# Loading w1 in two parts instead of four runs, with a new instruction order, in a fused S5 scan and gated MLP kernel

## The chip, the cores and the metric

The kernel runs on one core of one Trainium2 chip. The metric is the time of one execution on the device, in microseconds (us); the median of the runs counts. One execution is also recorded by the hardware profiler; its span, from the first to the last instruction, is shorter than the time of the whole execution, which has some start and end around it.

The engines have their own instruction streams and run in order: PE (TensorE, matrix products; PEld is its weight load), DVE (VectorE), ACT (ScalarE), POOL (GpSimd) and SP (SyncE, which here only issues DMAs). An instruction that waits for a semaphore holds back everything behind it on its own engine.

## What is computed

The reference, cut to its core (L = 2048 rows, D = 448, F = 1792, all inputs bf16):

```python
xn = layernorm(x)
# part A: a diagonal complex state of size 448, scanned over the rows
Lam_bar = exp(exp(log_dt) * (Lambda_re + 1j * Lambda_im))
Bu = xn @ (((Lam_bar - 1) / Lam)[:, None] * (B_re + 1j * B_im)).T
h[t] = Lam_bar * h[t - 1] + Bu[t]
s = 2 * (h @ (C_re + 1j * C_im).T).real + xn * Dskip
# part B: an MLP on a second layernorm
g = silu(gelu(layernorm(xn) @ w1 + b1) @ w2 + b2)
out = x + s * g
```

## The kernel before, in words

The rows go through in 4 groups of 512, each group in 2 blocks of 256 rows; a block holds 128 pairs of an even and an odd row. A group passes through these stages, named here as in the rest of the text, with their lines:

- **Layernorm.** DVE takes statistics (L395, L401; for group 0 L425, L426), then scales: for group 0 ACT makes the first ones (L428 and L429), for the others POOL or DVE makes a power or a Newton step (L472 to L482, the last of them L482). DVE or ACT normalizes into `xn_sb` for part A and `xn2_sb` for part B (L447 for group 0; L493 on DVE, L494 on ACT). Both are transposed to `xnT` and `xn2T`, by transposing DMAs on SP (L83), except that group 0's part B is transposed on TensorE (L454) and copied from PSUM by DVE or ACT (L413).
- **mm1** (L803). xn2T times w1, 14 column tiles of 128 ("tiles of F") taken in pairs, each pair in two phases of 6 and 8 matmuls. K is 448, so the last 64 rows of K are handled by a second copy: `w1_sb` has in its fourth plane the rows 384 to 447 in partitions 64 to 127, and in partitions 0 to 63 a copy of rows 320 to 383 that DVE makes (L350). A phase needs its PSUM banks free: ACT drains each pair with gelu into `gT` (L807), and those drains come in TensorE's order. Group 0 goes through five pairs for block 0 first, then the pairs 5 and 6 for both blocks, then five pairs for block 1.
- **mm2** (L828). gT times w2, 14 matmuls for each of four quarters of a group, in PSUM banks 5 and 6. DVE adds b2 (L831), ACT applies silu (L833), or tanh (L835) with a DVE step (L836) for the groups in the middle. ACT loads a table when it changes between gelu (L620), silu and sine (L616).
- **The state.** TensorE makes Bu (L731) from xnT and BT, four steps of two products each per group, in bank 4; ACT or DVE copies it to `u_sb` (L413). DVE rotates it (L746 to L750), scans it (L755, twice, and L757), ACT or DVE copies the scan to bf16 (L413, `vs`), DVE rotates back (L773 to L777) into `h_sb`; L777 is the last step, of the half pair of states.
- **y** (L871, L874, L877). h times CZ (even rows, with xn times M0 added) or CQ (odd rows), in bank 7. DVE adds the skip term (L883) and multiplies by g (L885, L888), DVE or POOL adds x (L891), SP stores.

Once, at the start, parameters are prepared: the rotation tables (DVE L626 to L633, then five sines on ACT, L642), the products LB of B (L660, L661, L663 into `Bn`), their transposes BT (DMA), the products CQ and CZ of C (L660, L661, L663), and M0 (L714, L699), which needs all seven CQ, with `De`, the identity times Dskip (L612), added. De lies in the scan's work space and so waits for the last of the sines. The b2 and Dskip rows are loaded by POOL's queue and wait for the last 64-row load of w1.

**The order is written out.** Every step is a task that says which names it reads and writes; `emit` derives the waits from them. `ORDER` lists all tasks in the order in which they are put on their engines' streams, so it alone sets what comes behind what on an engine and on SP's and POOL's queues. `SECOND` lists the tasks that take their second engine (of DVE, ACT and POOL). DMAs have a semaphore each; a reader waits until the whole transfer has landed. SP's queue is in order: a transpose that waits for its source holds back the loads behind it.

**The loads of w1.** `CH` cuts the 14 tiles into runs of 2, 4, 4 and 4. `ldw1(c, ...)` loads run c: one transfer for the rows 0 to 383 (384 row pieces, name `w1_c`), one for the rows 384 to 447 (`w1r_c`), and the copy of 64 rows (`w1c_c`). A phase of mm1 reads the names of its run. SP issues, in this order: x of block 0 (odd half, even half), x of block 1, the 64 rows of run 1, run 1, run 0, its 64 rows, the 64 rows of run 2, run 2, run 3, its 64 rows, x of blocks 2 and 3, the four pieces of w2, and then B and C in turn.

Of the kernel before, what the change touches and what calls it, by code (L numbers as in the profile page):

```python
# [7 lines left out]
ACT = mybir.ActivationFunctionType  # L8
# [145 lines left out]
def dram_ap(t, offset, ap):  # L154
    return bass.AP(tensor=t.tensor, offset=offset, ap=ap)
# [2 lines left out]


ORDER = [int(k) for k in """  # L160
# [17 lines left out]
""".split()]  # L178
SECOND = [int(k) for k in """
46 54 55 62 64 67 70 75 77 84 108 113 131 134 159 161 163 164 166 178 185 186 188 190 191 221 223 225 227 229 231 239 249 250 259 267 269 330 361 363  # L180
364 383 399 400 435 446 467 479 481 486 490 498 500 501 503 509 527 528 608 611
""".split()]


# [14 lines left out]
def bass_recurrent_scan__ssm_conv_s5__mixer_channel_mlp__prompt_kernel(  # L199
# [18 lines left out]
    with ExitStack() as es:  # L218
# [85 lines left out]
        with nc.Block():  # L304
# [26 lines left out]
            def ld(eng, o, i, writes, nbytes, prio, reads=(), dur=0.45):  # L331
                kb.dma(eng, o, i, reads=reads, writes=writes, prio=prio, nbytes=nbytes, dur=dur)
# [9 lines left out]
            CH = ((0, 2), (2, 4), (6, 4), (10, 4))  # L342
            chunk = [c for c, (_, n) in enumerate(CH) for _ in range(n)]

            def ldw1(c, prio):
                a, w = CH[c][0] * 128, CH[c][1] * 128
                ld("sp", w1_sb[:, 0:3, a:a + w], dram_ap(B_w1, a, [[F, 128], [128 * F, 3], [1, w]]), [f"w1_{c}"], 384 * w * 2, prio, dur=0.55)
                ld("sp", w1_sb[64:128, 3, a:a + w], dram_ap(B_w1, 384 * F + a, [[F, 64], [1, w]]), [f"w1r_{c}"], 64 * w * 2, prio)
                low, high = w1_sb[0:64, 3, a:a + w], w1_sb[64:128, 2, a:a + w]
                kb.either(("dve", lambda e: e.tensor_copy(low, high)), ("act", lambda e: e.activation(low, high, ACT.Copy)), [f"w1_{c}"], [f"w1c_{c}"])  # L350

            S1 = 10 * PINNED
            for par in range(0 if 0 else 2):
                ld("sp" if par or not 0 else "act", x_all[:, 0, par, :], dram_ap(A_x, par * D, [[2 * D, 128], [1, D]]), [f"x0p{par}"], 114688, S1)
            ldx(1, 1, S1 + 2)
            ldw1(0, S1 + 1)
            ld("pool", brows[0:3, :], dram_ap(B_b1, 256, [[512, 3], [1, 512]]), ["br0"], 3072, 0, reads=["br"])
            ld("pool", brows[3:4, 0:256], dram_ap(B_b1, 0, [[256, 1], [1, 256]]), ["br1"], 512, 0, reads=["br"])
            for c in (1, 2, 3):
                ldw1(c, S1 + 3)  # L360
            for ri, bm in enumerate((A_B_re, A_B_im)):
                ld("sp", Bn[:, ri * 3:ri * 3 + 3, D:896], dram_ap(bm, 0, [[D, 128], [128 * D, 3], [1, D]]),
                   [f"Bn{ri}"], 344000, S1 + 5, dur=0.9)
# [494 lines left out]
            def ym(g, b, par, prio):  # L858
# [9 lines left out]
                def part(c0, c1):  # L868
                    bk = 7 if g < NG - 1 else (7, 4, 0)[(2 * b + par + (c0 > 0)) % 3]
                    w = c1 - c0  # L870
                    fns = [lambda e, k=k: e.matmul(psum[:, bk, c0:c1], h_sb[:, hb, k, k0:k0 + 128], cm[:, k, c0:c1], start=(k == 0), stop=False)  # L871
                           for k in range(7)]
                    if par == 0:
                        fns += [lambda e, d=d: e.matmul(psum[:, bk, c0:c1], xnT[:, gx, d, xs], M0[:, d, c0:c1], start=False, stop=(d == 3)) for d in range(4)]  # L874
                        du, rk = 2.1, [f"M0{d}" for d in range(4)] + [f"M0{d}d" for d in range(3)] * 1 + [f"CZ{k}" for k in range(7)]
                    else:
                        fns[-1] = lambda e: e.matmul(psum[:, bk, c0:c1], h_sb[:, hb, 6, k0:k0 + 128], cm[:, 6, c0:c1], start=False, stop=True)  # L877
                        du, rk = 1.36 * w / D + (0.05 if w < D else 0), [f"CQ{k}" for k in range(7)]
                    pe(fns, [f"h{hb}", f"hh{hb}", f"hp{hb}"] + ([f"xnT{gx}_{b}"] if par == 0 else []) + rk, [f"ps{bk}"], du, prio + c0 / 1e4)
                    y, ky = psum[:, bk, c0:c1], f"ps{bk}"  # L880
                    if par and not late(n):
                        y, ky = xr[:, b, c0:c1], f"xr{b}"
                        dve(lambda e: e.tensor_tensor(xr[:, b, c0:c1], psum[:, bk, c0:c1], xd[:, g % 2 * 2 + b, c0:c1], ALU.add), [f"ps{bk}", f"xd{g % 2 * 2 + b}"] + ([f"CZ{k}" for k in range(7)] if g == 0 else []), [ky])  # L883
                    if silu_now(g):
                        dve(lambda e: e.scalar_tensor_tensor(out=t3[:, fb, c0:c1], in0=y, scalar=2.0, in1=g_sb[:, gs, c0:c1],  # L885
                                                             op0=ALU.mult, op1=ALU.mult), [ky, f"g{gs}"], [f"t3{fb}_{c0}"])
                    else:
                        dve(lambda e: e.tensor_tensor(t3[:, fb, c0:c1], y, g_sb[:, gs, c0:c1], ALU.mult), [ky, f"g{gs}"], [f"t3{fb}_{c0}"])  # L888
                    far = par and late(n)
                    res = xr[:, b, c0:c1] if far else x_all[:, 2 * g + b, par, c0:c1]  # L890
                    add = lambda e: e.tensor_tensor(o_sb[:, ob, par * D + c0:par * D + c1], t3[:, fb, c0:c1], res, ALU.add)  # L891
                    rd = [f"t3{fb}_{c0}", f"t3{fb}_256"] if c0 == 0 and not (last and par) else [f"t3{fb}_{c0}"]
                    rd += [f"xr{b}"] if far else xk(2 * g + b)
                    on = [("dve", add, 0.1 + (0.28, 0.47)[par] * w / D, 0.12), ("pool", add, 0.2 + 1.1 * w / D, 0.15)]
                    if last and par or 1:
                        kb.either(*on, rd, [f"o{ob}_{par}_{c0}"], prio)
                    else:
                        dve(add, rd, [f"o{ob}_{par}_{c0}"], on[0][2], prio)
                    if last:
                        kb.dma("act" if c0 else "sp", dram_ap(out, off + par * D + c0, [[2 * D, 128], [1, w]]), o_sb[:, ob, par * D + c0:par * D + c1], reads=[f"o{ob}_{par}_{c0}"],  # L900
                               writes=[f"out{g}{b}{par}{c0}"], prio=prio, nbytes=256 * w)
# [119 lines left out]
```

## Time and profile before

| | us |
|---|---|
| median of 3 runs | 153.87 (153.40 to 154.16) |
| the profiled execution, whole | 154.72 |
| its span, first to last instruction | 153.0 |
| PE busy | 147.5 |
| DVE busy | 128.3 |
| ACT busy | 98.4 |
| POOL busy | 40.5 |

Of the span, mm1 (L803) has TensorE busy for 44.7 us, mm2 (L828) for 44.4, Bu (L731) for 24.0. The granted TensorE clock is 1.0 throughout.

How to read the lines in this text. A line of the timeline gives start, length, engine, line, operation, output from inputs, shape, and in brackets the idle time before it with what ended it. A line of the chain of waits gives start, length and what the end of the program was waiting for in that stretch. A group's line gives the count, busy time, mean duration in ns, and the idle time before. A line of the DMA view gives the size of a transfer and the time from its issue to its landing. Instructions of one engine overlap a little, so ends are later than the next start by up to 0.1 us on DVE and ACT.

### The profile page before, as it was taken

The page shows a single profiled execution, that of the slowest core. Times are in us where ns is not written, and L with a number is a line of the kernel's source. Part 1 is how long each engine was busy: PE and PEld are TensorE (multiplying, and loading weights), DVE is VectorE, ACT ScalarE, POOL GpSimd, SP SyncE. Part 2 cuts the span into 40 slices and gives each one's busy share as a digit, 9 for nine tenths or more (in the row PEclk, how much of TensorE's full clock was granted, in tenths as well). Part 3 has the DMA queues.
Part 4 walks back from the last instruction along what each step waited for, and adds up shares of the span by engine and source line. Part 5 has one row for each costly group of instructions (what it writes and reads, how often), then busy time and mean ns, then how long its engine had stood idle before and what let it go on. Part 6 is the DMA issues. An engine that isn't in the chain of part 4 may idle for free.

```text
span 153.0 us, 2990 instructions
## 1 busy us (share of the span) xinstructions
PE 147.5 (96%) x1136; PEld 87.4 (57%) x1136; DVE 128.3 (84%) x270; ACT 98.4 (64%) x182; POOL 40.5 (26%) x100
## 2 busy tenths in 40 slices
PE   7979999999999999999999999999999999999992
PEld 7767755544566567545544556764454666555551
DVE  2839988999998969999999996469968726999984
ACT  3785998968889739997898620453479834067400
POOL 5267843135020920000447006200072031000200
DMA  4899999979996300600003031710331001100022
GB/s 119 239 276 398 282 216 185 182 152 144 170 237 170 58 4 0 132 5 4 0 0 62 4 60 30 167 48 16 60 93 29 4 0 57 63 0 0 4 99 81
DMA packets 31236, 14.73 MB, mean 96 GB/s; under 512 B 24752, under 2 KB 30774, under 8 KB 31222
## 3 DMA queue, kind: packets, MB, share of 16 engines
q1 hardware_dynamic: 30912, 14.26, 40.8%
q0 software_dynamic: 160, 0.23, 0.7%
q8 instruction: 9, 0.15, 0.4%
q10 hardware_dynamic: 150, 0.05, 0.1%
q14 instruction: 5, 0.04, 0.1%
HBM read 6.89 MB, written 1.84 MB: 57 GB/s over the span
## 4 chain that ended last, share of the span: by engine, by line
PE 92%; DMA 3%; DVE 1%; SPq 1%; issue 1%; DVEq 0%
PE psum L803 29%; PE psum L828 28%; PE psum L731 14%; PE psum L871 12%; PE psum L874 4%; DMA w_sb<-in_B_w_dram 3%; PE psum L714 3%; SPq L84 1%; PE psum L877 1%; DVE t L885 1%; DVE tmp L891 1%; PE psum L699 1%; PE psum L454 0%; DVEq L136 0%
## 5 line engine op out<-in xcount | busy, mean ns | idle before, releaser
L803 PE MATMUL psum<-xn2T,w_sb 64*128 64x512 bf16 (+1 forms) x462 | 44.7, 345 | 1.3 <-issue 0.9
L828 PE MATMUL psum<-w_sb,gT 128*128 128x448 bf16 x224 | 44.4, 353 | 0.0
L807 ACT ACTIVATE gT<-psum,b1f 128x512 bf16<-128x512 f32 (+1 forms) x66 | 36.0, 624 | 11.7 <-PE psum L803 11.5
L803 PEld LDWEIGHTS psum<-xn2T,w_sb 64*128 64x128 bf16 x462 | 24.3, 109 | 20.8 <-issue 3.1
L828 PEld LDWEIGHTS psum<-w_sb,gT 128*128 128x128 bf16 x224 | 21.6, 98 | 20.3 <-issue 0.6
L413 ACT ACTIVATE u_sb<-psum 128x512 bf16<-128x512 f32 (+2 forms) x22 | 10.5, 477 | 23.0 <-PE psum L731 22.7
L731 PE MATMUL psum<-xnT,BT 128*128 128x256 bf16 x196 | 24.0, 273 | 0.0
L731 PEld LDWEIGHTS psum<-xnT,BT 128*128 128x128 bf16 x196 | 19.0, 98 | 5.4 <-issue 1.1
L755 DVE TENSOR_TENSOR_SCAN s_w<-dk,vs 128x774 f32<-128x774 f32 x8 | 14.0, 1760 | 0.1
L891 POOL TENSOR_TENSOR tmp<-t,x_all 128x448 bf16<-128x448 bf16 x5 | 5.2, 1032 | 33.1 <-DVE t L888 30.7
L494 ACT ACTIVATE xn_sb<-x_all,lnw 128x448 bf16<-128x448 bf16 (+2 forms) x21 | 13.0, 661 | 1.2 <-DVE xn_sb L493 1.1
L413 ACT ACTIVATE vs<-s_w 64x256 bf16<-64x256 f32 (+2 forms) x16 | 10.9, 682 | 2.6 <-DVE s_w L755 1.5
L871 PE MATMUL psum<-CZ,h_sb 128*128 128x448 bf16 x56 | 11.9, 352 | 0.0
L831 DVE TENSOR_TENSOR o<-psum,b2bc 128x448 f32<-128x448 f32 x16 | 9.8, 615 | 1.2 <-PE psum L828 1.0
L871 PE MATMUL psum<-CQ,h_sb 128*128 128x448 bf16 (+2 forms) x54 | 10.5, 332 | 0.0
L871 PEld LDWEIGHTS psum<-CZ,h_sb 128*128 128x128 bf16 x56 | 5.4, 98 | 4.7 <-DVE lnmv L401 0.4
L871 PEld LDWEIGHTS psum<-CQ,h_sb 128*128 128x128 bf16 x54 | 5.1, 98 | 4.0 <-DVE t L885 0.4
L874 PE MATMUL psum<-M,xnT 128*128 128x448 bf16 x32 | 7.4, 352 | 0.0
L883 DVE TENSOR_TENSOR Cr<-psum,xd 128x448 f32<-128x448 f32 x7 | 4.3, 620 | 3.5 <-PE psum L877 3.4
L395 DVE BATCH_NORM_STATS2 lnst<-x_all 128x6 f32<-128x448 bf16 x12 | 7.0, 615 | 0.2 <-DMA x_all<-in_A_x_dram 0.2
L474 POOL TENSOR_TENSOR lnw<-lnw,mhalf 128x8 f32<-128x8 f32 x3 | 7.0, 2335 | 0.2
L493 DVE TENSOR_SCALAR xn_sb<-x_all,lnw 128x448 bf16<-128x448 bf16 (+2 forms) x19 | 6.9, 396 | 0.0
(160 smaller groups left out, 188.7 us busy)
## 6 DMA issues: line engine op xcount, KB each, us to landing
out_dram<-tmp SPq DMA_DIRECT2D x7, 224.0 KB, 2.0
x_all<-in_A_x_dram SPq DMA_DIRECT2D x3, 448.0 KB, 4.1
w_sb<-in_B_w_dram SPq DMA_DIRECT2D x3, 448.0 KB, 8.6
w_sb<-in_B_w_dram SPq DMA_DIRECT2D x3, 384.0 KB, 6.1
vs<-in_A_C_re_dram SPq DMA_DIRECT2D x1, 392.0 KB, 11.2
Bn<-in_A_B_im_dram SPq DMA_DIRECT2D x1, 336.0 KB, 10.0
Bn<-in_A_B_re_dram SPq DMA_DIRECT2D x1, 336.0 KB, 10.2
vs<-in_A_C_im_dram SPq DMA_DIRECT2D x1, 336.0 KB, 10.2
```

The costliest lines, as they stand in the source:

```text
L395: dve([lambda e, b=b, par=par, q=q: e.bn_stats(lnst[:, q, :], x_all[:, 2 * g + b, par, :])], [f"x{2 * g + b}"] , [f"st{q}"], 0.62, prio)
L413: kb.either(("act", [lambda e, o=o, i=i: e.activation(o, i, ACT.Copy) for o, i in pairs]), ("dve", [lambda e, o=o, i=i: e.tensor_copy(o, i ...
L474: power = fns + [lambda e: e.tensor_tensor(w(2), w(0), mhalf[:].to_broadcast([128, 2, nq]), ALU.pow), lambda e: e.tensor_tensor(w(3), mean ...
L494: ("act", [lambda e, o=o, i=i: e.activation(o, i, ACT.Identity, bias=nb, scale=rs) for o, i in parts], 0.75, 0.2)]
L731: fns = [lambda e, r=r, m=m, d=d: e.matmul(psum[:, 4, r * NK:(r + 1) * NK], BT[:, m, d, :], xnT[:, gx, d, :], start=(d == 0), stop=(d == 6 ...
L755: dve(lambda e, so=so, vi=vi: e.tensor_tensor_scan(so, dk[:].rearrange("p i c -> p (i c)"), vi, 0.0, ALU.mult, ALU.add), ["v", "vl", "dk", ...
L803: return lambda e: e.matmul(view(bk[k]), w1_sb[rows, d, fcol(2 * j + k)], rhs[rows, d, :, :], start=not second and n == 0, stop=second and ...
L807: act([lambda e, k=k: e.activation(gT[:, gb, 2 * j + k, :].rearrange("p (r c) -> p r c", r=2)[:, :, cols], view(bk[k]), ACT.Gelu_apprx_tan ...
L828: fns = [lambda e, fi=fi: e.matmul(psum[:, bk, 0:D], gT[:, gb, fi, q * 128:(q + 1) * 128], w2_sb[:, fi, :], start=(fi == 0), stop=(fi == N ...
L831: dve(lambda e: e.tensor_tensor(o2[:, fb, :], psum[:, bk, 0:D], b2bc[:], ALU.add), [f"ps{bk}", "b2bc"], [f"oo{fb}"], 0.62, prio - 76)
L871: fns = [lambda e, k=k: e.matmul(psum[:, bk, c0:c1], h_sb[:, hb, k, k0:k0 + 128], cm[:, k, c0:c1], start=(k == 0), stop=False) for k in ra ...
L874: fns += [lambda e, d=d: e.matmul(psum[:, bk, c0:c1], xnT[:, gx, d, xs], M0[:, d, c0:c1], start=False, stop=(d == 3)) for d in range(4)]
```

## The change

`ldw1` now takes several runs at once and is called for the runs 0 and 1 (6 tiles of F) and for the runs 2 and 3 (8 tiles). Each call makes one transfer of 384 rows and one of 64 rows, so there are 4 transfers for w1 instead of 8, with row pieces of 1,536 and 2,048 bytes instead of 512 and 1,024. The names stay, so a phase of run 0 or 1 now waits for both, and likewise for 2 and 3. The four copies of 64 rows stay as they are. `LW` is the list of the two parts.

```diff
-            def ldw1(c, prio):
-                a, w = CH[c][0] * 128, CH[c][1] * 128
-                ld("sp", w1_sb[:, 0:3, a:a + w], dram_ap(B_w1, a, [[F, 128], [128 * F, 3], [1, w]]), [f"w1_{c}"], 384 * w * 2, prio, dur=0.55)
-                ld("sp", w1_sb[64:128, 3, a:a + w], dram_ap(B_w1, 384 * F + a, [[F, 64], [1, w]]), [f"w1r_{c}"], 64 * w * 2, prio)
...
+            def ldw1(cs, prio):
+                a, w = CH[cs[0]][0] * 128, sum(CH[c][1] for c in cs) * 128
+                ld("sp", w1_sb[:, 0:3, a:a + w], dram_ap(B_w1, a, [[F, 128], [128 * F, 3], [1, w]]), [f"w1_{c}" for c in cs], 384 * w * 2, prio, dur=0.55)
+                ld("sp", w1_sb[64:128, 3, a:a + w], dram_ap(B_w1, 384 * F + a, [[F, 64], [1, w]]), [f"w1r_{c}" for c in cs], 64 * w * 2, prio)
+                for c in cs:
+                    a, w = CH[c][0] * 128, CH[c][1] * 128
...
+            LW = ((0, 1), (2, 3))
...
-            ldw1(0, S1 + 1)
+            ldw1(LW[0], S1 + 1)
...
-            for c in (1, 2, 3):
-                ldw1(c, S1 + 3)
+            for cs in LW[1:]:
+                ldw1(cs, S1 + 3)
```

There are 628 tasks instead of 632, and `ORDER` and `SECOND` are new throughout:

```diff
 ORDER = [int(k) for k in """
-1 14 20 0 48 10 17 19 21 15 2 95 28 18 96 92 27 93 22 16 25 49 5 97 13 109 94 91 110 98 105 104 26 106 100 23 99 50 51 56 6 52 66 107 3 111 101 112 57
...
+18 1 17 0 19 10 16 44 2 20 14 45 88 91 5 21 92 89 96 15 87 22 26 93 105 106 90 46 101 23 102 94 47 100 97 27 48 108 52 49 95 104 103 107 51 110 28 98
...
```

With the numbers put back to tasks, what moves is this:

- **SP** issues x of block 0 (even half, odd half), x of block 1, the 6-tile part, its 64 rows, the 8-tile part, its 64 rows, x of blocks 2 and 3, the four pieces of w2, the three pieces of C, then the transpose of group 1's second xn2T block, Bn1, Bn0, Bn60, a transpose of C (Ct0), Bn61, the transpose of group 1's first xn2T block, and so on with transposes of C, xnT and B mixed in another order. Before, all loads of B and C came ahead of the first transpose, and both blocks of xn2T were its first two.
- **TensorE**, group 0: the same phases of mm1, pairs 0, 1, 2 instead of 1, 2, 0 first; the 8 transposes of block 1 come ahead of pair 2's second phase; the first mm2 quarter (14 matmuls) comes ahead of the last three phases of mm1. Later: some mm2 quarters change places with each other or with a Bu step; in group 3 the last Bu step comes ahead of its neighbouring mm2 quarter; an mm2 quarter of group 2 moves from behind mm1 of group 3 to ahead of it.
- **ACT** normalizes block 2 for part B in group 1's preparation (L494, two pieces of two instructions), the first piece ahead of three drains of gT, and the odd half of block 1 for part A; before, it did three pieces for part A there, behind the first of these drains.
- **DVE** takes both statistics of block 0 ahead of their aggregates, and the three pieces for part A that ACT did; its own three (two of block 2 for part B, one of block 1 for part A) are the ones that ACT takes. De's second part (L612) moves from among the products CQ to ahead of most products LB.
- **DVE, group 3's state**: L888 of another quarter between the two scans, L749 ahead of the first scan, L831 of a quarter behind the second scan, L750, L891 and L757 too (in the time of ACT's copy), an L891 between the two first products of the back rotation, and L883 of a y step ahead of L776 and L777. The third copy of u on this path (L413) goes from ACT to DVE.
- **Engines.** About 65 tasks change their engine, most of them small parameter steps between POOL and DVE; in all DVE has 9 tasks more, ACT one more, and POOL 10 fewer.

More of the change, by code (lines that the diff above doesn't have):

```diff
@@ L160 @@
 ORDER = [int(k) for k in """
[17 rows of a table removed]
[17 rows of a table added]
 """.split()]
 SECOND = [int(k) for k in """
-46 54 55 62 64 67 70 75 77 84 108 113 131 134 159 161 163 164 166 178 185 186 188 190 191 221 223 225 227 229 231 239 249 250 259 267 269 330 361 363
-364 383 399 400 435 446 467 479 481 486 490 498 500 501 503 509 527 528 608 611
+42 49 58 60 62 64 67 71 74 76 77 78 80 84 86 104 127 130 153 154 155 156 157 161 174 182 183 184 186 193 217 219 221 223 225 229 237 246 255 256 257
+263 265 329 345 348 349 357 359 360 374 395 398 431 435 439 444 445 463 482 496 500 503 520 521 526 571 584 604
 """.split()]
@@ L343, in bass_recurrent_scan__ssm_conv_s5__mixer_channel_mlp__prompt_kernel @@
             chunk = [c for c, (_, n) in enumerate(CH) for _ in range(n)]
-            def ldw1(c, prio):
-                a, w = CH[c][0] * 128, CH[c][1] * 128
-                ld("sp", w1_sb[:, 0:3, a:a + w], dram_ap(B_w1, a, [[F, 128], [128 * F, 3], [1, w]]), [f"w1_{c}"], 384 * w * 2, prio, dur=0.55)
-                ld("sp", w1_sb[64:128, 3, a:a + w], dram_ap(B_w1, 384 * F + a, [[F, 64], [1, w]]), [f"w1r_{c}"], 64 * w * 2, prio)
-                low, high = w1_sb[0:64, 3, a:a + w], w1_sb[64:128, 2, a:a + w]
-                kb.either(("dve", lambda e: e.tensor_copy(low, high)), ("act", lambda e: e.activation(low, high, ACT.Copy)), [f"w1_{c}"], [f"w1c_{c}"])
+            def ldw1(cs, prio):
[4 more added lines that the diff above has]
+                    a, w = CH[c][0] * 128, CH[c][1] * 128
+                    low, high = w1_sb[0:64, 3, a:a + w], w1_sb[64:128, 2, a:a + w]
+                    kb.either(("dve", lambda e, low=low, high=high: e.tensor_copy(low, high)), ("act", lambda e, low=low, high=high: e.activation(low, high, ACT.Copy)), [f"w1_{c}"], [f"w1c_{c}"])
+            LW = ((0, 1), (2, 3))
             S1 = 10 * PINNED
@@ L874, in part @@
                         fns += [lambda e, d=d: e.matmul(psum[:, bk, c0:c1], xnT[:, gx, d, xs], M0[:, d, c0:c1], start=False, stop=(d == 3)) for d in range(4)]
-                        du, rk = 2.1, [f"M0{d}" for d in range(4)] + [f"M0{d}d" for d in range(3)] * 1 + [f"CZ{k}" for k in range(7)]
+                        du, rk = 2.1, [f"M0{d}" for d in range(4)] + [f"M0{d}d" for d in range(3)] + [f"CZ{k}" for k in range(7)]
                     else:
```

32 rows, old and new, of the table ORDER are left out of this document.

## The prediction

> **What bounds the kernel now.** I read the page first, then the chain of work that ended last, then each engine's timeline where that chain changes hands.
>
> ```profile
> span 153.0 us, 2990 instructions
> PE   7979999999999999999999999999999999999992
> GB/s 119 239 276 398 282 216 185 182 152 144 170 237 170 58 4 0 132 5 4 0 0 62 4 60 30 167 48 16 60 93 29 4 0 57 63 0 0 4 99 81
> ```
>
> TensorE is full in all but the first, third and last slice: a change gains only where TensorE still waits, and costs wherever it makes TensorE wait. The chain in order of time (start, length, what):
>
> ```profile
> 7.16 2.69 PE psum L803 x42
> 9.85 0.55 PE psum L454 x8
> 10.40 0.89 issue
> 11.29 7.49 PE psum L803 x104
> ...
> 20.47 10.70 PE psum L828 x56
> 31.17 10.04 PE psum L803 x90
> ...
> 49.65 1.32 PE psum L714 x7
> ```
>
> Before 7.16 nothing of L803 can run. At 10.40 it stops for 0.89, and starts again when the second half of w1 is there. After 11.29 the chain stays on TensorE to the end, but for small pieces. The loads' own rows, each asked for in the window of its issue (size, time from issue to landing):
>
> ```profile
> w_sb<-in_B_w_dram SPq DMA_DIRECT2D x1, 384.0 KB, 4.3
> w_sb<-in_B_w_dram SPq DMA_DIRECT2D x1, 192.0 KB, 4.7
> w_sb<-in_B_w_dram SPq DMA_DIRECT2D x1, 384.0 KB, 6.1
> w_sb<-in_B_w_dram SPq DMA_DIRECT2D x1, 64.0 KB, 6.3
> x_all<-in_A_x_dram SPq DMA_DIRECT2D x1, 448.0 KB, 6.8
> ```
>
> These were issued at 2.80 (run 1), 3.42 (run 0), 5.13 (run 2), 6.29 (the 64 rows of run 3) and 6.83 (x of blocks 2 and 3). So they landed at 7.1, 8.1, 11.2, 12.6 and 13.6.
>
> **The change part by part.** The sum is made against the profiled execution: its span is 153.0, its own time 154.72; the median of the runs shown is 153.87. A difference found in the span is added to the median.
>
> *(1) The start of L803.* SP now issues block 0's even half before its odd half, DVE takes both statistics first, and ACT makes both scales one behind the other.
>
> ```profile
> 2.91 0.63 DVE L425 BATCH_NORM_STATS2 lnst<-x_all 128x6 f32<-128x448 bf16 x1 [1.61 <-DMA x_all<-in_A_x_dram]
> 3.91 0.63 DVE L425 BATCH_NORM_STATS2 lnst<-x_all 128x6 f32<-128x448 bf16 x1 [0.16 <-DMA x_all<-in_A_x_dram]
> 4.67 0.36 DVE L447 TENSOR_SCALAR xn_sb<-x_all,lnmv,lnw 128x448 bf16<-128x448 bf16 x1
> 6.54 0.39 DVE L413 COPY xn2T<-psum 128x512 bf16<-128x512 bf16 x1
> 4.79 0.29 ACT L428 ACTIVATE lnw<-lnmv,eps 128x1 f32<-128x1 f32 x1 [0.42 <-DVE lnmv L426]
> ```
>
> Before, the first scale was made while DVE waited for the second half, and the first normalize ran at 4.67. Now both aggregates come after the second statistics (4.54), so the two scale pairs (0.53 each: the 0.29 shown, 0.20 for L429 behind it, and the gap) run from 4.8 to 5.8. The normalizes end at about 6.2 instead of 5.87, and DVE gains a small product (0.16) ahead of the copy to xn2T, which ends near 7.4 instead of 6.93. L803 starts near 7.5 instead of 7.16: +0.35. The weights must be there too. The 6-tile load and its 64 rows carry the same bytes as the old runs 0 and 1, which had landed at 7.1 and 8.1; I take 7.5, nearer the first row, as it is issued first and in one piece; ends 7.1 and 8.4. So this costs +0.35 (0 to +1.2).
>
> *(2) The gap at 10.40.* TensorE does the same 42 matmuls and 8 transposes first: 2.69 + 0.55 after 7.5 is 10.75. The 8-tile load (768 KB and 128 KB) then has to be there whole, where before run 2 alone opened the way at 11.2. At the 276 GB/s of the third slice its 0.92 MB end 3.3 us after the first load (10.8), at the 398 GB/s of the fourth 2.3 after (9.8); the old last row is 12.6. I take 11.0, near the third slice's rate, in whose time it runs; the ends are 9.8 and 12.6. Against 11.29: -0.3 (-0.5 to +1.3), with the loss of (1) already in it. DVE's two copies of 64 rows come together behind it, then the two copies to xn2T of block 1: 1.1 us by their old spacing, while TensorE has 20 matmuls (1.2 us) that need neither, so no wait. On POOL the b2 load, which waits for the same 64 rows, has the sine steps behind it; POOL comes to it near 11.8 by its own list, so it is covered.
>
> The Trainium skill (DMA: Bandwidth & Descriptors, "Bandwidth", measured table) has it that transfers should be batched to 1 MiB or more, small ones being dominated by descriptors. By that rule the four fewer transfers are a plain gain, which is a rival below.
>
> *(3) The first mm2 pass.* The new TensorE order puts the first 14 matmuls of L828 ahead of the last three L803 phases, which before waited on ACT's drains: 22 matmuls from 18.78 to 20.47, against 1.25 at the pace of the 42. That hides 0.4. But ACT now has block 2's normalize (two pieces) ahead of three gelu drains, and it waits for DVE's scale of group 1:
>
> ```profile
> 13.62 2.21 DVE L395 BATCH_NORM_STATS2 lnst<-x_all 128x6 f32<-128x448 bf16 x4
> ...
> 19.66 0.17 DVE L482 SCALAR_TENSOR_TENSOR lnw<-lnmv,lnw 128x8 f32<-128x8 f32 x1
> ```
>
> DVE needs 6.2 us from the statistics to that row, and by the new list 6.1. With x of blocks 2 and 3 at 13.2 (0.4 earlier, one of the gains of fewer issues ahead; ends 12.5 and 13.6) ACT starts the piece at 19.3, ends it at 20.3 and has the waiting drain done at 21.2, just when the moved matmuls end (18.45 + 2.65 = 21.1). So TensorE is through with mm2 at 30.4 instead of 31.17: -0.75 (-1.2 to +0.4).
>
> *(4) The second L803 run.* Most of this is given back, since ACT has become the later one there.
>
> ```profile
> 18.79 2.06 ACT L494 ACTIVATE xn_sb<-x_all,lnw 128x448 bf16<-128x448 bf16 x3
> 20.74 2.29 ACT L807 ACTIVATE gT<-psum,b1f 128x256 bf16<-128x256 f32 x6
> 23.11 1.28 ACT L616 ACT_TABLE_LOAD   x1
> 31.94 0.58 ACT L833 ACTIVATE g_sb<-o 128x448 bf16<-128x448 f32 x1 [1.04 <-DVE o L831]
> 32.59 1.28 ACT L620 ACT_TABLE_LOAD   x1
> 33.97 1.27 ACT L807 ACTIVATE gT<-psum,b1f 128x512 bf16<-128x512 f32 x2
> ```
>
> Before, ACT had 14.2 us of work from 18.07 (the last drain ahead of these rows) to 33.88 and idled 1.6, most of it the 1.04 shown. The new list has 14.7: two normalize pieces of 1.0 and one of 0.7 for the three of 2.06, and one product of Bn in another's place. From 19.3 without an idle it is through with the gelu table at 34.0, as before. The first drain of L803 is over at 35.2. TensorE, which starts at 30.6 (the second transposed load of xn2T lands there, below), needs that bank after 42 matmuls of 0.108, at 35.15; the next drain at 36.35 makes it wait 0.5. At the first L731 it stands at 40.95 against 41.14: -0.2 in all.
>
> SP moves count here: the first transpose of xn2T is now issued before three of Bn's four loads, and waits on SP for DVE (20.3); Bn's loads, before from 10.05 on, wait behind it and are issued at 22 to 24.
>
> ```profile
> xn2T<-xn_sb SPq DMA_TRANSPOSE x1, 4.5
> Bn<-in_A_B_re_dram SPq DMA_DIRECT2D x1, 336.0 KB, 10.2
> ```
>
> The other xn2T transpose follows Bn and one of Cr at 26.1; with 4.5 it lands at 30.6. Bn's 10.2 was spent behind a full queue, which the DMA has worked off by 22. I take 4 us, like the 384 KB row, landing near 27; ends 25 and 34.
>
> *(5) DVE up to M0.* Its products of Bn start at 27; then an identity product (L612, moved forward by 11 us of DVE work, with L831 of the last mm2 block behind it) waits for ACT's last sine, at 31.0, which covers a landing up to 27.3 (3.7 us of work lie between). From there the new list has 18.1 us to the last of CQ: 49.1.
>
> L714 (quoted above) needs all seven CQ, at 49.45 by (4): covered by 0.3. The remaining swaps between DVE, ACT and POOL up to 128 us have such covers too, most over 1 us, some (the M0 copies, u of the third block, an xr of group 0) 0.1 to 0.3. I allow +0.2 for all of these (0 to +1.5).
>
> *(6) The last state chain.* Between the last pair of u (128.35) and hh, DVE's work sets when TensorE may start the last y.
>
> ```profile
> 132.35 1.77 DVE L755 TENSOR_TENSOR_SCAN s_w<-dk,vs 128x774 f32<-128x774 f32 x1
> 136.34 1.49 ACT L413 ACTIVATE vs<-s_w 128x1536 bf16<-128x1536 f32 x1 [1.30 <-DVE s_w L755]
> 142.40 0.29 DVE L777 TENSOR_TENSOR h_sb<-pa 128x256 bf16<-128x256 bf16 x1
> 142.95 1.30 PE L871 MATMUL psum<-CQ,h_sb 128*128 128x448 bf16 x6
> ```
>
> hh is done at 142.69 and used at 142.95: 0.26 spare. The groups of this stretch have these sizes:
>
> ```profile
> L888 DVE TENSOR_TENSOR t<-psum,g_sb 128x448 bf16<-128x448 f32 x1 | 0.6, 618 | 0.0
> L749 DVE TENSOR_TENSOR pa<-u_sb,WT 128x512 bf16<-128x512 bf16 x1 | 0.4, 418 | 0.0
> L891 DVE TENSOR_TENSOR tmp<-t,x_all 128x448 bf16<-128x448 bf16 x1 | 0.4, 384 | 0.0
> ```
>
>  From one start to the next, overlaps counted, the new list puts into this stretch L888 between the scans (+0.65), L749 ahead of them (+0.35), an L891 (+0.4) and an L883 as large as L888, which before came after hh (+0.6). It takes out L831 between the scans (-0.5) and, behind ACT's copy, L750, L891 and L757 (-1.15). What it does during ACT's copy is 2.0 against 1.5 (+0.45). Sum +0.8, less 0.26: TensorE waits 0.55 before its last y (0 to 0.9). As the chain starts from TensorE's own L731, no earlier shift takes this away. The tail behind the last matmul keeps its order.
>
> Sum: -0.2 + 0.2 + 0.55 = +0.55, or 153.87 + 0.55, rounded 154.5; own range 153.5 to 155.6 with the ends of (2) to (6) not all on one side.
>
> **The rivals.** *Bn's late loads become the bound (slower).* If the loads behind the xn2T transpose take 6.1, as w1's third run did, they land at about 29 and not 27, past the 27.3 from which it decides; DVE then ends CQ at 50.8, L714 waits 1.4 beyond its cover, and 155.9 comes out. With the 10.2 of Bn's own row it would be 5 us and 159. For it: DVE idled under 1 us in this stretch before and can't catch up. Against it: the queue is short by then.
>
> *The larger transfers gain what they promise (faster).* The first load is there by 7.1 and the second by 9.8; ACT's piece starts at 18.5, its table is ready at 33.2, and the second L803 run ends 0.75 earlier; if the last chain's spacing is also as tight as before, 153.0. This is what the batching rule of the Trainium skill cited above would make of it. For it: short rows of w1 are gone. Against it: the old eight transfers, from 2.2 to 12.6, already overlapped.
>
> *Nothing to be seen.* The same bytes pass and TensorE stays full from 11.3 on, with the last chain's excess hidden: 153.9.
>
> **How the numbers follow.** About 0.5% (0.77 us) is what a measurement of this kernel can tell from no change. Forecast 0.46 (0.30 of it within 0.5%, 0.15 slower, 0.01 faster); Bn late or another of the thin covers of (5) gone, 0.32, all slower; the faster rival 0.16 (0.14 faster, 0.02 within); nothing to be seen 0.06. That gives faster 0.15, same 0.38, slower 0.47. The likeliest case is 154.5; the range, 153.0 to 156.8, leaves out the 159 and the faster rival's better half.
>
> **What would show it.** The first L803 at 7.4 to 7.6; its stop before the second half under 0.4; mm2's first pass over at 30.4; a wait of L803 on gT of about 0.5 after 35; L714 not waiting; a TensorE gap of 0.4 to 0.7 before the last y, released by L777. Wrong would be L714 waiting on CQ, L731 on BT, or no gap at the end.

## The result and the profile after

| | before | after |
|---|---|---|
| median of 20 runs | 154.17 us (153.40 to 154.86) | 155.19 us (154.31 to 157.33) |
| ratio | | 1.007 (95%: 1.0048 to 1.0093) |
| the profiled execution, whole | 154.72 | 154.75 |
| its span | 153.0 | 153.0 |

The changed kernel is slower by 0.7%, about 1.0 us. Two of its 20 runs were slow ones (157.33, with a granted clock of 0.986, and 156.90) and are left out of the ratio; the median of the other 18 is 155.14. Yet the two profiled executions take the same time. Before's lies 0.55 above its own median of 20 runs, after's 0.44 below its own. So the difference can't be read from these two traces alone; it took further executions of both kernels.

From the page of the changed kernel: TensorE's busy share in 40 slices, then what the DMA moved.

```profile
span 153.0 us, 2977 instructions
PE   7899999999999999999999999999999999999992
GB/s 120 322 354 333 188 132 231 143 207 163 209 171 228 25 4 137 0 4 2 0 0 0 35 89 0 60 60 107 155 0 0 6 60 60 0 0 60 4 60 120
```

The bytes come earlier: the second and third slices move 322 and 354 GB/s, where before had 239 and 276 (in the further executions below 298 to 337 and 332 to 353, against 239 and 309). TensorE is as full as it was. The chain of waits of the changed kernel has moved, though (start, length, what):

```profile
4.42 7.43 DMA x_all<-in_A_x_dram
...
21.72 4.84 DMA Bn<-in_A_B_re_dram
...
33.54 2.43 ACT gT L811 x4
36.02 4.77 PE psum L807 x40
...
68.18 0.76 ACT xn_sb L498
68.94 1.38 ACT vs L417
70.78 1.28 ACT gT L811 x2
72.11 5.44 PE psum L807 x48
```

Before, this chain stayed on TensorE from 11.29 on. Now it runs through DMA, DVE and ACT up to 36, and again through ACT at 68 to 72: at both places TensorE has nothing in hand when another engine is late. (In e1, a second execution of the same kernel, the chain is on TensorE from 11.31 on, and only the second of these places is left.) The loads' rows of the changed kernel (size, time from issue to landing); the last is the second b1 load, on POOL's queue:

```profile
w_sb<-in_B_w_dram SPq DMA_DIRECT2D x1, 768.0 KB, 7.1
w_sb<-in_B_w_dram SPq DMA_DIRECT2D x1, 576.0 KB, 4.4
dk<-in_B_b_dram POOLq DMA_DIRECT2D x1, 0.5 KB, 4.2
```

TensorE's timeline at the start of the changed kernel:

```profile
6.87 0.27 PE L600 MATMUL psum<-ident,dk 4*128 4x3 bf16 x4 [0.43 <-DMA dk<-in_B_b_dram]
7.01 0.18 PE L601 MATMUL psum<-ident,dk 4*128 4x1 bf16 x2
7.12 0.45 PE L420 MATMUL psum<-ones 128*128 128x128 bf16 x5
7.51 2.03 PE L807 MATMUL psum<-xn2T,w_sb 64*128 64x256 bf16 x34
9.48 0.62 PE L458 MATMUL psum<-ident,xn_sb 128*128 128x128 bf16 x8
10.03 0.63 PE L807 MATMUL psum<-xn2T,w_sb 64*128 64x256 bf16 x8
10.99 1.27 PE L807 MATMUL psum<-xn2T,w_sb 64*128 64x256 bf16 x19 [0.34 <-issue]
```

There are two stops to see. L600 turns b1 into columns and waits for the b1 load; five dummies (L420) stand behind it, so mm1 (L807) starts at 7.51. It then uses up the first part and stops until 10.99, when the 64 rows of the second part are there too (issued at 3.88, 7.0 to their landing).

### The profile page after: what moved, and what is told of

The parts are those of the page before. It is cut to its first block, busy times and chain, and to the rows that moved or that the text cites. A ratio compares the mean times of both kernels' runs of the same rounds, so it can differ in the third digit from the quotient of the medians.

```text
span 153.0 us, 2977 instructions
## 1 busy us (share of the span) xinstructions
PE 147.5 (96%) x1136; PEld 87.3 (57%) x1136; DVE 129.3 (84%) x281; ACT 97.1 (63%) x182; POOL 38.0 (25%) x89
## 4 chain that ended last, share of the span: by engine, by line
PE 69%; DVE 9%; DMA 8%; ACT 7%; SPq 3%; issue 2%; DVEq 0%; ACTq 0%
PE psum L832 19%; PE psum L807 16%; PE psum L735 14%; PE psum L875 12%; DMA x_all<-in_A_x_dram 5%; PE psum L878 4%; DMA Bn<-in_A_B_re_dram 3%; PE psum L718 3%; SPq L84 3%; ACT gT L811 2%; DVE lnst L399 1%; DVE xn_sb L497 1%; ACT vs L417 1%; ACT tmp L664 1%; PE psum L881 1%
## 5 line engine op out<-in xcount | busy, mean ns | idle before, releaser
L807 PE MATMUL psum<-xn2T,w_sb 64*128 64x512 bf16 (+1 forms) x462 | 44.8, 345 | 0.7 <-issue 0.3
L807 PEld LDWEIGHTS psum<-xn2T,w_sb 64*128 64x128 bf16 x462 | 24.6, 109 | 20.0 <-ACT gT L811 2.7
L498 ACT ACTIVATE xn_sb<-x_all,lnw 128x384 bf16<-128x384 bf16 (+2 forms) x25 | 14.9, 638 | 1.0 <-DVE h_sb L779 0.9
L875 PE MATMUL psum<-CZ,h_sb 128*128 128x448 bf16 x56 | 11.9, 353 | 0.0
L835 DVE TENSOR_TENSOR o<-psum,b2bc 128x448 f32<-128x448 f32 x16 | 9.8, 617 | 1.9 <-PE psum L832 1.7
L417 ACT ACTIVATE vs<-s_w 64x256 bf16<-64x256 f32 (+2 forms) x9 | 6.7, 767 | 4.9 <-DVE s_w L759 4.8
L770 POOL TENSOR_TENSOR ang<-s_w,ang 128x16 f32<-128x16 f32 x2 | 1.2, 576 | 33.4 <-ACT s_w L768 18.6
L837 ACT ACTIVATE g_sb<-o 128x448 bf16<-128x448 f32 x8 | 4.4, 568 | 5.8 <-DVE o L835 5.7
```

The source lines that it names most:

```text
L417: kb.either(("act", [lambda e, o=o, i=i: e.activation(o, i, ACT.Copy) for o, i in pairs]), ("dve", [lambda e, o=o, i=i: e.tensor_copy(o, i ...
L498: ("act", [lambda e, o=o, i=i: e.activation(o, i, ACT.Identity, bias=nb, scale=rs) for o, i in parts], 0.75, 0.2)]
L807: return lambda e: e.matmul(view(bk[k]), w1_sb[rows, d, fcol(2 * j + k)], rhs[rows, d, :, :], start=not second and n == 0, stop=second and ...
L835: dve(lambda e: e.tensor_tensor(o2[:, fb, :], psum[:, bk, 0:D], b2bc[:], ALU.add), [f"ps{bk}", "b2bc"], [f"oo{fb}"], 0.62, prio - 76)
```

## The experiments

Every ratio is against runs of the kernel before on the same chip, with its 95% interval. For each profiled execution two times say most: when mm1 starts, and when it goes on with the second half of w1 ("second half"). What lies behind the second half is called the rest: the whole time of the profiled execution less that moment.

| kernel | mm1 starts | second half | rest | profiled, whole | ratio |
|---|---|---|---|---|---|
| before | 7.16 | 11.29 | 143.43 | 154.72 | |
| before again (e2) | 6.85 | 9.98 | 143.69 | 153.67 | 0.9996 |
| after | 7.51 | 10.99 | 143.76 | 154.75 | 1.0070 |
| after again (e1) | 7.43 | 11.31 | 143.56 | 154.87 | 1.0074 |
| after again (e4) | 7.70 | 11.05 | 144.35 | 155.40 | 1.0069 |
| after again (e3) | 8.77 | 11.75 | 143.86 | 155.61 | 1.0061 |
| e5, two parts, old order | 8.18 | 11.31 | 143.38 | 154.69 | 1.0043 |
| e6, four runs, new order | 7.04 | 10.51 | 144.91 | 155.42 | 1.0108 |
| e7, first part whole | 8.78 | 11.77 | 143.52 | 155.29 | 1.0049 |
| e8, second part whole | 7.68 | 11.74 | 143.45 | 155.19 | 1.0062 |
| e9, ACT's piece later | 7.53 | 11.85 | 143.52 | 155.37 | 1.0053 |
| e10, e7 with b1 behind | 7.14 | 10.53 | 143.70 | 154.23 | 1.0056 |
| e11, mm2 back | 8.06 | 11.24 | 144.90 | 156.14 | 1.0126 |
| e12, four runs, old start | 7.28 | 10.67 | 144.82 | 155.49 | 1.0081 |

**e1 to e4: both kernels again.** The kernels that ran as e1, e3 and e4 are the changed kernel, unaltered, and e2 is the kernel before, unaltered. The edits that the expectations of e1, e2 and e3 speak of are not in them, so these three texts are not tested by these runs; the first two edits are made in e5 and e6, and Bn's loads were never moved. The runs count as further executions.

> The two-part loads of w1 in the order of before (the 6-tile load and its 64 rows where runs 1 and 0 were issued, the 8-tile load and its rows where runs 2 and 3 were). Theory (the new order costs, because three loads of Bn now sit behind a transpose and land with no slack): the loads alone change nothing or gain a little, ratio 0.996 to 1.002, TensorE's stop at 10.4 shrinks from 0.89 to about 0.4. Rival (the larger transfers themselves arrive less evenly and hold back the small loads on the other queue): ratio 1.005 to 1.009 here, with single runs up to 157.

> The four-run loads of w1 as before in the new order. Theory: the order carries the cost, ratio 1.005 to 1.010, single runs over 156. Rival (the transfers): ratio 0.998 to 1.002, and no run over 155.5.

> The changed kernel with the four loads of Bn issued right behind Cn, ahead of the transpose of xn2T that they were queued behind. Theory: Bn lands by about 20, DVE no longer waits for it at 26.7, the runs scatter less (highest under 156) and the ratio falls to 0.999 to 1.003. Rival (ACT comes late to the gelu drains of the third block run, and the last chain): the ratio stays at 1.005 to 1.009 and the scatter stays.

> The changed kernel once more, nothing altered, for its scatter and for a second profiled execution. Both theories: ratio 1.005 to 1.009. If its profiled execution is over 155.5, the place where it loses against the first profile tells them apart: at DVE's wait for Bn and the first products behind it by the theory, in the third block run by the rival.

Measured: after 155.32, 155.10 and 155.20 (12 runs each; ratios 1.0074, 1.0061 and 1.0069, all intervals within 1.0033 to 1.0099), before 153.84 (0.9996, 0.9972 to 1.0021). So the loss is the same each time. The theory named for e4, that a slower execution loses its time at DVE's wait for Bn, fell: the rest is not longer in e3, the slowest (155.61), than in the first profile by more than 0.1 (e4's is, by 0.6, but at w2, shown below). Its rival, the third block run, fell too: that run takes 10.40 to 10.41 in all four executions of the changed kernel and 9.87 to 9.88 in both of before, a fixed loss of 0.5. What the slower executions lose against the first, they lose in the first 20 us. TensorE in e3:

```profile
8.13 0.27 PE L600 MATMUL psum<-ident,dk 4*128 4x3 bf16 x4 [1.66 <-DMA dk<-in_B_b_dram]
8.27 0.18 PE L601 MATMUL psum<-ident,dk 4*128 4x1 bf16 x2
8.38 0.45 PE L420 MATMUL psum<-ones 128*128 128x128 bf16 x5
8.77 2.03 PE L807 MATMUL psum<-xn2T,w_sb 64*128 64x256 bf16 x34
```

Here b1 came 1.3 later still, and mm1 started at 8.77. In e4 another load was late, w2, for the first 14 matmuls of mm2 that the new order has put ahead of three phases of mm1:

```profile
19.18 2.81 PE L832 MATMUL psum<-w_sb,gT 128*128 128x448 bf16 x14 [0.73 <-DMA w_sb<-in_B_w_dram]
```

And the second execution of before shows what its first had hidden. TensorE in e2:

```profile
6.85 2.65 PE L803 MATMUL psum<-xn2T,w_sb 64*128 64x256 bf16 x42 [0.20 <-DVE xn2T L413]
9.43 0.62 PE L454 MATMUL psum<-ident,xn_sb 128*128 128x128 bf16 x8
9.98 2.27 PE L803 MATMUL psum<-xn2T,w_sb 64*128 64x256 bf16 x32
```

There is no stop before the second half: the four runs can arrive in time. The row of the three larger ones in e2:

```profile
w_sb<-in_B_w_dram SPq DMA_DIRECT2D x3, 384.0 KB, 4.2
```

It said 6.1 in before's first execution. The stop of 0.89 at 10.40, on which the forecast built its one gain at the start, is there in one of two executions of the kernel and not in the other. Averaged over four and two executions, after's second half starts at 11.28 (10.99, 11.31, 11.05, 11.75) and before's at 10.64, so 0.64 later; the rest is 143.88 against 143.56, so 0.32 longer. Together 0.96, near the 1.02 between the medians. The two executions of before lie 1.31 apart at the second half, so this split is rough; the medians of e5 below are the firmer ground.

**e5 and e6: the loads and the order apart.** e5 has the two parts in the old order (w1's first part and its 64 rows in the places of runs 1 and 0, the second part in those of runs 2 and 3), e6 the four runs in the new one. Numbers are those of the changed kernel's tasks (22 and 28 are the two parts, 23 and 29 their 64 rows).

```diff
 e5, the start of SP's list; all engines' lists likewise
-19 20 21 22 23 28 29 43 38 37 39 36 203
+20 19 21 22 23 28 29 43 39 37 38 36 35
 e6
-            LW = ((0, 1), (2, 3))
+            LW = ((0,), (1,), (2,), (3,))
```

> The two-part loads of w1 in the whole old order (the 6-tile load and its 64 rows where runs 1 and 0 were issued, the 8-tile load and its rows where runs 2 and 3 were; all else as before). Theory: the loss comes from the second part, which must land whole before its first tile can be used: TensorE resumes L807 at 10.9 to 11.4, against 9.98 where the four runs arrived in good time (11.29 where they did not), and the ratio is 1.004 to 1.009 with the old order too. Rival (the new order, Bn's late loads above all, carries the loss): ratio 0.997 to 1.002.

> The new order with w1 in four runs again, issued 0, 1, 2, 3, all where the two parts were issued. Theory: L807 resumes near 10, the ratio is 0.996 to 1.002. Rival of the order: 1.005 to 1.010, with Bn's landing and DVE's wait at 26.7 as in the changed kernel.

Measured: e5 154.62, ratio 1.0043 (1.0024 to 1.0062); e6 155.44, ratio 1.0108 (1.0079 to 1.0138). The loads alone cost 0.66 us (0.0043 of 154.05; 0.4 to 1.0 by the interval), as the theory had it, and in the profiled execution they cost it at the start: e5's rest is that of before. TensorE in e5:

```profile
7.93 0.27 PE L599 MATMUL psum<-ident,dk 4*128 4x3 bf16 x4 [1.09 <-DMA dk<-in_B_b_dram]
...
8.18 2.49 PE L806 MATMUL psum<-xn2T,w_sb 64*128 64x256 bf16 x42
10.60 0.62 PE L457 MATMUL psum<-ident,xn_sb 128*128 128x128 bf16 x8
11.31 1.95 PE L806 MATMUL psum<-xn2T,w_sb 64*128 64x256 bf16 x30
```

Two things come together at 11.31: mm1 had started late (8.18), behind b1, and the 64 rows of the second part landed at 11.2 (issued at 3.89, 7.3 to their landing), as the theory said.

e6 came out as the rival had it in its ratio, but not by the rival's mechanism. Its second half starts early (10.51), and then the new order works against the old loads. DVE in e6:

```profile
9.73 0.29 DVE L351 COPY w_sb<-w_sb 64x512 bf16<-64x512 bf16 x1 [1.15 <-DMA w_sb<-in_B_w_dram]
11.22 0.29 DVE L351 COPY w_sb<-w_sb 64x512 bf16<-64x512 bf16 x1 [1.20 <-DMA w_sb<-in_B_w_dram]
11.43 0.74 DVE L416 COPY xn2T<-psum 128x512 bf16<-128x512 bf16 x2
```

The new order has both copies of 64 rows of the second half ahead of block 1's copies to xn2T. With one part both come at once, at 10.37; with four runs the second waits for run 3, the xn2T copies wait behind it, and TensorE waits for them at 12.27. The old order has the xn2T copies ahead of run 3's, so the kernel before is spared this. But TensorE in e6 stops a second time, for w2:

```profile
12.27 0.95 PE L806 MATMUL psum<-xn2T,w_sb 64*128 64x512 bf16 x8 [0.48 <-DVE xn2T L416]
...
19.32 2.81 PE L831 MATMUL psum<-w_sb,gT 128*128 128x448 bf16 x14 [0.76 <-DMA w_sb<-in_B_w_dram]
```

Without the first stop it would only have stood longer at the second, so this execution does not show what the first one costs (e12 does), and e6 does not measure the order by itself. By the ratios, the new order costs less with the loads that it was made for: against the kernel before, the new loads in the old order lose 0.43%, both together 0.70%, and the old loads in the new order 1.08% (the last two intervals overlap).

**e7 and e8: one part whole, the other in runs**, in the new order.

```diff
 e7
-            LW = ((0, 1), (2, 3))
+            LW = ((0, 1), (2,), (3,))
 e8
-            LW = ((0, 1), (2, 3))
+            LW = ((0,), (1,), (2, 3))
```

> The changed kernel with its first part of 6 tiles whole and the 8 tiles behind it in two runs of 4. Theory (the second part's wholeness costs): L807 resumes by 10.4 and the ratio falls to 0.998 to 1.003. Rival (the first part costs, as it comes 0.3 to 1.4 later and holds back the small b1 load, for which TensorE waits ahead of L807): the start stays at 7.4 to 8.8 and the ratio at 1.004 to 1.008. Rival of the order: unchanged at 1.007.

> The changed kernel with its first 6 tiles in two runs of 2 and 4 as before (the run of 2 first) and the 8-tile part whole. Theory: b1 lands earlier and L807 starts at 7.0 to 7.3, but the resume stays at 10.9 to 11.4 and the ratio at 1.004 to 1.008. Rival of the first part: 0.998 to 1.003. Rival of the order: unchanged at 1.007.

Measured: e7 154.57, 1.0049 (1.0022 to 1.0075); e8 154.79, 1.0062 (1.0034 to 1.0091). Neither gives the loss back, and the intervals reach over the changed kernel's 1.007. So e7 came out as its rival had it and not as the theory, and e8 in its ratio as the theory. The traces say why one half alone doesn't help. In e7 run 2 is there early, but b1 and the first part's 64 rows are late (both 5.5 from issue to landing) and mm1 starts at 8.78. In e8 b1 is on time (3.0), mm1 starts at 7.68, and then TensorE waits for the second part:

```profile
10.29 0.63 PE L806 MATMUL psum<-xn2T,w_sb 64*128 64x256 bf16 x8
11.74 1.52 PE L806 MATMUL psum<-xn2T,w_sb 64*128 64x256 bf16 x22 [0.82 <-DMA w_sb<-in_B_w_dram]
```

The second half starts at 11.77 in the one and 11.74 in the other. It comes 2.98 to 2.99 behind the start of mm1 (e3 and e7), or when the second part has landed (e1, e4, e8), whichever is later. In these executions each part's wholeness delays one of the two.

**e9 to e12: single terms, and an attempt at a better version.** e9 moves one normalize piece of ACT behind the gelu drains of the third block run. e10 is e7 with TensorE's b1 columns, and ACT's copy of them, behind the first two phases of mm1. e11 puts the first 14 matmuls of mm2 back behind the last three phases of mm1. e12 has the new order with four runs issued as before, TensorE's first phases as before, and e9's move. Again in the changed kernel's numbers, cut to one engine:

```diff
 e9, ACT
-243 445 344 346 407 413 410 416 422 424 394
+243 344 346 407 413 410 416 422 424 445 394
 e10, PE
-100 108 103 110 111 114 115 112 129
+100 103 110 111 108 115 112 114 129
 e11, PE
-141 271 147 145 150 268
+141 147 145 150 271 268
 e12, PE, beside e9's move and LW = ((0,), (1,), (2,), (3,))
-103 110 111 114 115 112
+103 111 114 115 110 112
```

> The changed kernel with one piece of ACT's normalize (xn_sb, 0.76 us at 68.18) moved behind the six pairs of gelu drains of the third block run, whose consumer is a transpose needed after 85. Theory: TensorE's waits in that run (0.26, 0.12 and 0.12 in the phases at 71.20, 76.71 and 80.76) go, all of the 0.5 stays gained to the end, ratio 1.002 to 1.005. Rival (ACT's copy of the scan, 1.47, is what is late, or the time is given back at a later drain): under 0.15 gained at 85, ratio 1.006 to 1.008.

> The kernel with only the first part whole (ratio 1.0049), and TensorE's b1 columns (L600, L601), ACT's copy of them and the wait for the b1 load moved behind the first two phases of L807. Theory: L807 starts when the first part's 64 rows are there, 0.1 behind their landing instead of 0.5, so 0.4 earlier than there; ratio 1.000 to 1.003. Rival (b1's wait was only standing where the rows would have held TensorE anyway): start and ratio as there, 1.004 to 1.006.

> The changed kernel with the first 14 matmuls of L832 back behind the last three L807 phases on TensorE, nothing else moved. Theory (those 14 now come before w2 has landed, and that wait of 0 to 0.8 eats what they hide): no wait on w2 at 18, but waits of 0.8 to 1.3 on the drains instead, as ACT's normalize pieces stay ahead of them; ratio 1.006 to 1.011. Rival (the wait on w2 is the order's whole loss): ratio 1.001 to 1.004.

> The new order with w1 in four runs issued as before (the 64 rows of run 1, run 1, run 0, its rows, ...), TensorE's first L807 phase on run 1 as before, and ACT's piece later as above. Theory (the start and the third block run carry the loss; the rest of the new order is even): L807 starts at 6.8 to 7.2 and resumes by 10.2, ratio 0.997 to 1.002, perhaps under both kernels. Rival (the order loses elsewhere, at w2 above all): 1.004 to 1.008.

Measured: e9 154.77, 1.0053 (1.0031 to 1.0076). The timeline of ACT, and then of TensorE, in the changed kernel:

```profile
68.18 0.76 ACT L498 ACTIVATE xn_sb<-x_all,lnw 128x448 bf16<-128x448 bf16 x1
68.85 1.47 ACT L417 ACTIVATE vs<-s_w 128x1536 bf16<-128x1536 f32 x1
...
70.78 2.42 ACT L811 ACTIVATE gT<-psum,b1f 128x512 bf16<-128x512 f32 x4
```

```profile
68.17 10.47 PE L807 MATMUL psum<-xn2T,w_sb 64*128 64x512 bf16 x90
78.57 1.50 PE L875 MATMUL psum<-CZ,h_sb 128*128 128x448 bf16 x7
```

and the same two in e9:

```profile
69.03 1.49 ACT L416 ACTIVATE vs<-s_w 128x1536 bf16<-128x1536 f32 x1
...
71.40 2.42 ACT L810 ACTIVATE gT<-psum,b1f 128x512 bf16<-128x512 f32 x4 [0.44 <-PE psum L806]
```

```profile
69.02 10.23 PE L806 MATMUL psum<-xn2T,w_sb 64*128 64x512 bf16 x90
79.19 1.50 PE L874 MATMUL psum<-CZ,h_sb 128*128 128x448 bf16 x7
```

In the kernel before, TensorE has:

```profile
68.59 9.94 PE L803 MATMUL psum<-xn2T,w_sb 64*128 64x512 bf16 x90
78.47 1.49 PE L871 MATMUL psum<-CZ,h_sb 128*128 128x448 bf16 x7
```

So the third block run takes 9.88 before (68.59 to the y behind it at 78.47), 10.40 after, and 10.17 in e9 and in e12, which has the same move. Without the piece ACT stands waiting for TensorE (0.44) and not the other way round; half of the 0.5 comes back, not all of it as the theory had it. In the medians 0.25 us can't be told from nothing with these intervals.

e10: 154.97, 1.0056 (1.0034 to 1.0079), beside e7's 1.0049. mm1 does start 0.13 after the part's 64 rows are there instead of 0.5 to 0.6, and its one profiled execution, with 154.23 the fastest of its runs, has the earliest second half of all kernels with a whole first part (10.53). The median doesn't follow: the forecast of 0.4 fell, and the rival, that the rows hold TensorE anyway, fits the ratio.

e11: 156.03, 1.0126 (1.0101 to 1.0150), as the theory had it and a little beyond. TensorE in e11:

```profile
20.10 1.39 PE L806 MATMUL psum<-xn2T,w_sb 64*128 64x256 bf16 x22 [1.46 <-ACT gT L810]
21.42 2.82 PE L831 MATMUL psum<-w_sb,gT 128*128 128x448 bf16 x14
```

The 14 matmuls do hide ACT's lateness, about 1.5 us as ACT's pieces now lie. They pay for it with w2's wait in some executions, 0.73 in e4 and 0.25 in e3.

e12: 155.37, 1.0081 (1.0054 to 1.0107). The start came as expected (7.28), the second half at 10.67 and not 10.2, and then the same conflict as in e6: DVE holds the xn2T copies behind run 3's rows, and TensorE waits 0.73 for them, here with no wait for w2 behind it. From the second half to mm2's first matmul 8.25 pass, against 7.33 in the changed kernel (10.99 to 18.32). At 37.01 a wait of 0.32 for ACT's drains follows. The rival's ratio came true, but not by a loss at w2. No version that ran beats the kernel before.

## Why the prediction came out as it did

The forecast was 0.55 above before's median; measured is 1.02. Slower by over 0.5% was the likeliest of its three classes, and 155.19 lies in the range, but partly for other reasons than the steps gave: between the two profiled executions, on which the sum was made, the change was worth 0.0 and not 0.55. That the forecast came this near is in part luck.

**The base of the sum failed.** "A difference found in the span is added to the median" held the profiled execution to be a typical one. It was a late one at just the place where step (2) counted its gain. Against 11.29 the second part's 10.99 is a gain of 0.3; against the 9.98 of the other execution it is a loss of 1.0. The runs showed a loss of 0.64 on average, and e5 shows 0.66 for the loads alone. The median moved too: 153.87 was that of three runs, and 20 gave 154.17, which is 0.30 of the distance from 154.5 to 155.19. The step's own number, 11.0 for the second part, was near: 10.99, 11.31, 11.05 and 11.75.

**Step (1), the start.** 7.5 was forecast and 7.51 measured, by another cause. The statistics' order cost nothing: DVE's copy to xn2T was done in time, and b1's load was late instead, which the prediction had not on its list of loads. Over four executions the start is 7.43 to 8.77, mean 7.85; the step was mis-sized by 0.35 and its upper end, 8.36, was passed once. What it said of the weights was near: the first part's 64 rows, for which it took 7.5 with ends of 7.1 and 8.4, landed at 7.0, 6.9, 7.1 and 8.2 (after, e1, e4, e3). So b1 is not the whole of it: in e3 the rows would have held mm1 until 8.2 without b1.

**Step (3), mm2's first pass.** Forecast over at 30.4, measured 30.45 in the profile, 30.78, 31.30 and 31.61 in the others. The hiding was real (e11), but the prediction asked only what the moved matmuls wait for on ACT, and not whether w2 has landed when they now start. x of blocks 2 and 3 landed at 11.9 (4.42 and 7.43 in the chain above), before the 12.5 that the step took as its early end.

**Steps (4) and (5).** TensorE's wait behind the gelu table was 0.2 where 0.5 was forecast, and in e1, e3 and e4 there was none. The rival of Bn's late loads did not come: its load landed when forecast, near 27. DVE's timeline shows the first product of Bn, and the groups of TensorE show M0 (count, busy, mean ns, idle before):

```profile
26.69 0.46 DVE L665 TENSOR_SCALAR tmp<-Bn,cw 128x448 f32<-128x448 bf16 x1 [0.50 <-DMA Bn<-in_A_B_re_dram]
```

```profile
L718 PE MATMUL psum<-CQ,Bn 128*128 128x448 bf16 x21 | 4.5, 352 | 0.0
```

DVE waited 0.5 and TensorE not at all. It was not tried what earlier loads of Bn would bring. The +0.2 that (5) allowed for all swaps with thin covers was too little: the third block run costs 0.5 by itself, in every execution. In the first profile of the changed kernel TensorE comes to it 0.42 earlier than in that of before (68.17 against 68.59) and leaves it 0.10 later (78.57 against 78.47). Half of the 0.5 is ACT's piece ahead of it (e9, e12); which of the other moves makes the other half was not tried.

**Step (6), the last chain.** Forecast was a wait of 0.55 before the last y. DVE's and TensorE's timelines of the changed kernel:

```profile
142.62 0.29 DVE L781 TENSOR_TENSOR h_sb<-pa 128x256 bf16<-128x256 bf16 x1
```

```profile
143.02 1.30 PE L875 MATMUL psum<-CQ,h_sb 128*128 128x448 bf16 x6
```

The y has no wait in its brackets. hh is done at 142.91, 0.22 later than before and not 0.8, which the spare 0.26 covers. The two scans stand as far apart as before: the L892 that came between them takes the place of an L835 of nearly the same length (0.60). And behind ACT's copy the list turned out 0.5 shorter, where the sum had 0.15. A term of 0.55 that is not there, and two of 0.5 and more that were not counted (the third block run, the start against a typical execution), left a sum that lies in the range because they partly cancel; that is luck.

**The faster rival** was that the larger transfers gain what they promise. The bytes did come earlier, yet the second half started later on average (11.28 against 10.64), since a phase in this kernel waits for the whole transfer of its tiles. The Trainium skill, whose batching rule the prediction cites, has the opposite advice too (Perfetto Trace Analysis, "DMA Optimizations"): splitting transfers into smaller chunks may allow some to start sooner. The runs side with that advice as far as w1's first users go, by the 0.66 us of e5.

## What to carry to other kernels

Before a sum is built on one profile, place that execution among the kernel's own runs, and ask of every wait on a DMA whether it is there in a second execution; a gain against a late landing is no gain against the median. The larger transfers here moved their bytes sooner but released their first users later, and a small load on another queue, which TensorE needed first, came later too. An order made for one set of loads need not fit another (e6 and e12): before putting one half of a change back, look for what now stands behind a wait that used to be short.

## What the hardware showed beyond the expected

The second b1 load is 0.5 KB, on POOL's queue, and is issued 2.4 to 2.5 us into the program. It took 2.6 to 3.2 us to land in the five executions with the first 6 tiles in two runs (before 3.0, e2 2.6, e6 2.8, e8 3.0, e12 3.2), and 4.1 to 5.5 in the nine executions with a whole first part (4.2, 4.1, 4.4 and 5.5 in the four of the changed kernel). In all nine it landed 0.17 to 0.25 behind the 576 KB transfer, which SP had issued 0.24 to 0.34 ahead of it. So it cost such a load up to 2.9 us, and the spread of b1 is that of the large transfer, which took 4.2 to 5.6. The Trainium skill (DMA: Bandwidth & Descriptors, "Issuing engines are not separate DMA queues") says that transfers of all issuing engines run on the same DMA engines and interleave. The traces agree that the two queues are not independent; of interleaving they show little here, as the small load never landed ahead of the large one. What makes the 576 KB transfer take 4.2 in one execution and 5.6 in another stays open.
